# Working out the experts' order before the first expert stretch, and spreading the table steps behind it

## The chip, the cores and the metric

The kernel runs on one core of one Trainium2 chip. The time is device microseconds for one execution. A number given as the time of a kernel is the median of several executions; a profile is one execution with the hardware profiler on. Engines are named as the profile names them: PE (TensorE), DVE (VectorE), ACT (ScalarE), POOL (GpSimd), SP (SyncE). PEld is PE's weight load, which runs beside its matmuls.

## The reference, cut to what matters

Three layers follow one another. The first is attention with 2 batches, 8 heads, 768 tokens and 64 channels, where a query sees only keys of its own cluster. The second, which the change is in, is a mixture of 8 experts over N = 1536 tokens of D = 512 channels, one expert to a token. The third is a bilinear layer.

```python
logits = x @ w_gate
expert_idx = np.argmax(logits, axis=1)
...
for e in range(E):
    mask = expert_idx == e
    xe = x[mask]
    h = np.maximum(xe @ w1[e], 0.0)
    ye = h @ w2[e]
    out[mask] = gate_w[mask, None] * ye
...
a = x @ w_a
b = x @ w_b
return (a * b @ w_out)
```

## The kernel before, in words

**Attention, then routing.** The attention part runs unit by unit under a plan written out by hand. For each block of 128 tokens `route` finds every token's expert and its place among that expert's tokens, and keeps a running count per partition and expert in `run`. GpSimd scatters the rows of x by expert into `xs` in DRAM (`scatter`, L558). The last three blocks are not waited for: `place_mm` (L929) puts their rows of the first expert straight into PSUM (`x0t`) by matmuls with a matrix of places, beside the earlier rows, which sixteen matmuls with the identity add (L998).

**The expert stretches.** There are nine, in the order `SEQ` (L72) = 0, 1, 2, 7, 3, 8, 4, 5, 6. The numbers 0 to 6 are windows of up to 256 tokens of one expert, 7 is a tile of 128 rows for the expert with the fewest tokens, and 8 a tile of 128 rows for what an expert has beyond its window. A loop over the tiles that are left follows (L1301); it runs over none or some, by the counts. Which expert stands at which place is worked out on the chip by `tables` (L642): it sums `run` over partitions with one matmul (`cnt`), finds the expert with the fewest tokens, and writes `ri`: row 0 is the expert of each place, row 1 its first row in `xs`, row 2 its first column in the output `yt`. `wi` holds the same for stretch 8, `tab` the rest, and `aux` gets for each token's place its number and its gate, by twelve scatters of GpSimd (L779).

**A window** (`window`, L1088) computes h in eight blocks of 128 features, twelve matmuls each: the high and the low part of the weights with the high part of the input, and the high part with the low part of the input (`xh`, `xl`). Each block goes to a PSUM bank with the tag `h`, of which there are three. ACT rectifies it into `hh`, and DVE makes `hl`, the rest; then the bank is free. Then come eight blocks of y. A 128-row tile (`tile_of`, L1125) computes h with tokens on partitions in two banks, rectifies it into `hs` on ACT, and turns it by transposes (L1148) for its y.

**Weights.** Each expert's two matrices come in eight pieces of 512 KB. A piece is loaded by SP into one of four `raw` buffers (`piece_load`), cast by ACT into its high part `hi` and subtracted by DVE into its low part `lo` (`piece_parts`, L130); the load of piece n therefore waits for the `lo` of piece n - 4. There are twelve slots for parts. All queues work in the order in which the program issues.

**Ticks.** `tick` (L1203) is called sixteen times to a stretch, once to a block of h or y, and twice or once in a tile. At each tick it does one step of `tables` (a step ends at a `yield`), and splits pieces up to a number that leads the use by 6 pieces at first and by 10 at most. At tick 4 it calls `start_next(0)` (L1254): SP loads the expert numbers of the next two places from `ri` into registers, so that those weights can be loaded, and issues the load of the next window's rows, `xw`. The next window's transposes (`win_xt`, L1075), with `xh` by ACT and `xl` by DVE, are issued behind the y blocks that the last argument of `window` names. `load_ov` reads the output column from `ri` into registers of ACT and DVE at the second of these.

**PSUM.** With the expert stretches' pool (`mps`) the eight banks are: two for `xt`, two for `y`, three for `h`, one for the count (`rt`). In the last ticks of the stretches the pieces of the bilinear layer are split too. The bilinear stage begins with `split_y` (`yh`, `yl`), reads `aux`, and is bound by its matmuls.

Of the kernel before, what the change touches and what calls it, by code (L numbers as in the profile page):

```python
# [8 lines left out]
F32 = mybir.dt.float32  # L9
# [3 lines left out]
I32 = mybir.dt.int32  # L13
# [10 lines left out]
W = 256  # L24
# [5 lines left out]
def cluster_attention__then__moe__then__bilinear_kernel(  # L30
# [5 lines left out]
    DM, E = w_gate.shape  # L36
# [15 lines left out]
    NSLOT = NA + NB  # L52
# [8 lines left out]
    cp = pool(ctx, "const")  # L61
# [142 lines left out]
    ps = pool(st_aps, "attn_ps", space=PSUM)  # L204
# [434 lines left out]

    regs = {}  # L640

    def tables(rps, tp):  # L642


        tot = run[0]
        c = rps.tile([128, 512], F32, tag="rt", name="cnt")
        nc.tensor.matmul(c[:, 0:E], lhsT=ones, rhs=tot, start=True, stop=True)
        cnt = cp.tile([128, E], F32, name="cnts")
        nc.vector.tensor_copy(cnt, c[:, 0:E])

        m = cp.tile([128, 8], F32, name="wm")
        e1 = cp.tile([128, E], F32, name="we1")
        od = tp.tile([128, E], F32, name="od")
        nc.vector.tensor_reduce(out=m[:, 0:1], in_=cnt[:, 1:E], axis=AX.X, op=ALU.min)
        yield
        nc.vector.scalar_tensor_tensor(out=e1[:, 1:E], in0=cnt[:, 1:E], scalar=m[:, 0:1], in1=efirst[:, 0, 1:E],
                                       op0=ALU.is_le, op1=ALU.mult)
        nc.vector.tensor_reduce(out=m[:, 1:2], in_=e1[:, 1:E], axis=AX.X, op=ALU.max)
        yield
        nc.vector.tensor_scalar(out=m[:, 2:3], in0=m[:, 1:2], scalar1=-1.0, scalar2=float(E), op0=ALU.mult, op1=ALU.add)  # L660
        nc.vector.scalar_tensor_tensor(out=od, in0=ecol, scalar=m[:, 2:3], in1=ecol, op0=ALU.is_ge, op1=ALU.add)
        nc.vector.tensor_copy(od[:, E - 1:E], m[:, 2:3])
        yield
        ri = tp.tile([128, 3, E], I32, name="ri")
        nc.vector.tensor_copy(ri[:, 0, :], od)
        nc.vector.tensor_scalar(out=ri[:, 1, :], in0=od, scalar1=float(NTOK), scalar2=None, op0=ALU.mult)
        regs["ri"] = ri
        yield

        hot = tp.tile([128, E, E], F32, name="hot")  # L670
        t8 = tp.tile([128, E, E], F32, name="t8")
        o8 = tp.tile([128, 2, E], F32, name="o8")
# [58 lines left out]
        n = cp.tile([128, 2], F32, name="wn")  # L731
# [37 lines left out]
        for b in range(B):  # L769
            t = cp.tile([128, NT, E], F32, name=f"pt_{b}")  # L770
# [171 lines left out]
    for i in range(end + LAG):  # L942
# [31 lines left out]
        if i >= LAG:  # L974
            p, g, h, j = units[i - LAG]
# [19 lines left out]
    for d in range(DB):  # L995
        for a in range(2):
            o = W * (d % 2) + 128 * a
            nc.tensor.matmul(x0t[d // 2][:, o:o + 128], lhsT=x0[:, a, 128 * d:128 * d + 128], rhs=ident,  # L998
                             start=False, stop=False, skip_group_check=True)
    for d in range(DB):  # L1000
        place_mm(2, d)
    for t in range(NP):
# [14 lines left out]
    mp = pool(st_me, "moe")  # L1017
# [70 lines left out]
    def window(w, n, c0, tick, nxt, at):  # L1088
        hh, hl = [], []
        y = mps.tile([128, DB, W], F32, tag="y", name=f"y{w}")  # L1090
        for fb in range(FB):
            wh, wl = parts(c0 + fb // 2, DB)
            f0 = 128 * (fb % 2)
            hp_ = mps.tile([128, 512], F32, tag="h", name=f"h{w}_{fb}", bufs=3)
            seq = [(a_, xh[w], d) for d in range(DB) for a_ in (wh, wl)] + [(wh, xl[w], d) for d in range(DB)]
            for i, (a_, b_, d) in enumerate(seq):
                nc.tensor.matmul(hp_[:, 0:n], lhsT=a_[:, d, f0:f0 + 128], rhs=b_[:, d, 0:n],
                                 start=(i == 0), stop=(i == len(seq) - 1))
            th = mp.tile([128, W], F32R, tag=f"hh{fb}", name=f"hh{w}_{fb}")
            tl = mp.tile([128, W], F32R, tag=f"hl{fb}", name=f"hl{w}_{fb}")  # L1100
            nc.scalar.activation(out=th[:, 0:n], in_=hp_[:, 0:n], func=AF.Relu)
            nc.vector.scalar_tensor_tensor(out=tl[:, 0:n], in0=hp_[:, 0:n], scalar=0.0, in1=th[:, 0:n].bitcast(F32),
                                           op0=ALU.max, op1=ALU.subtract)
            hh.append(th)
            hl.append(tl)
            tick()
        for fb in range(FB):
            tick()
            wh, wl = parts(c0 + 4 + fb // 2, 2)
            for d in range(DB):  # L1110
                for i, (a_, b_) in enumerate(((wh, hh[fb]), (wh, hl[fb]), (wl, hh[fb]))):
                    nc.tensor.matmul(y[:, d, 0:n], lhsT=a_[:, fb % 2, 128 * d:128 * d + 128], rhs=b_[:, 0:n],  # L1112
                                     start=(fb == 0 and d % 2 == 0 and i == 0),
                                     stop=(fb == FB - 1 and d % 2 == 1 and i == 2), skip_group_check=True)
            if fb in at:
                nxt(at.index(fb))
        return y
# [6 lines left out]

    def tile_of(w, c0, tick, nxt, at):  # L1125

        hp_ = [mps.tile([128, 512], F32, tag="h", name=f"h{w}_{i}", bufs=3) for i in range(2)]
        hs = mp.tile([128, F], F32, tag="ys", name="hs", bufs=2)
        hh = [mp.tile([128, W], F32R, tag=f"hh{i}", name=f"sh{i}") for i in range(FB // 2)]
        hl = [mp.tile([128, W], F32R, tag=f"hl{i}", name=f"sl{i}") for i in range(FB // 2)]  # L1130

        def h_part(c):
            tick()
            tick()
            wh, wl = parts(c0 + c, DB)
            o = hp_[c // 2][:, 256 * (c % 2):256 * (c % 2) + 256]
            for d in range(DB):
                for i, (a_, b_) in enumerate(((xh[w], wh), (xl[w], wh), (xh[w], wl))):
                    nc.tensor.matmul(o, lhsT=a_[:, d, 0:WS], rhs=b_[:, d, :], start=(d == 0 and i == 0),
                                     stop=(d == DB - 1 and i == 2))  # L1140

        def h_split(i):
            nc.scalar.activation(out=hs[:, 512 * i:512 * i + 512], in_=hp_[i], func=AF.Relu)

        def h_turn(i):
            x = mps.tile([128, 512], F32, tag="xt", name=f"ht{i}", bufs=2)
            for j in range(4):
                nc.tensor.transpose(x[:, 128 * j:128 * j + 128], hs[:, 512 * i + 128 * j:512 * i + 128 * j + 128], ident)  # L1148
            for j in range(2):
                nc.scalar.copy(out=hh[2 * i + j], in_=x[:, W * j:W * j + W])  # L1150
            for j in range(2):
                nc.vector.tensor_tensor(out=hl[2 * i + j], in0=x[:, W * j:W * j + W],
                                        in1=hh[2 * i + j].bitcast(F32), op=ALU.subtract)

        y = mps.tile([128, DB, W], F32, tag="y", name=f"y{w}").rearrange("p d t -> p (d t)")[:, 0:512]

        def y_part(fb):
            tick()
            wh, wl = parts(c0 + 4 + fb // 2, 2)
            for i, (a_, b_) in enumerate(((hh, wh), (hl, wh), (hh, wl))):  # L1160
                nc.tensor.matmul(y, lhsT=a_[fb // 2][:, WS * (fb % 2):WS * (fb % 2) + WS], rhs=b_[:, fb % 2, :], start=(fb == 0 and i == 0),
                                 stop=(fb == FB - 1 and i == 2))

        h_part(0)
        h_part(1)
        h_split(0)
        h_part(2)
        h_turn(0)
        h_part(3)
        h_split(1)  # L1170
        y_part(0)
        y_part(1)
        h_turn(1)
        y_part(2)
        nxt(0)
        y_part(3)
        nxt(1)
        for fb in range(4, 8):
            y_part(fb)
        yn = mp.tile([128, F], F32, tag="ys", name="yn", bufs=2)[:, 0:DM]  # L1180
        nc.scalar.copy(out=yn, in_=y)

        def finish(a):
            if a:
                return
            x = mps.tile([128, 512], F32, tag="xt", name="yt_t", bufs=2)
            for d in range(DB):
                nc.tensor.transpose(x[:, 128 * d:128 * d + 128], yn[:, 128 * d:128 * d + 128], ident)
            store(x.rearrange("p (d t) -> p d t", d=DB), WS, at())

        return finish

    state = {"t": 0}
    LEAD = 6
# [8 lines left out]
    def tick():  # L1203
        t = state["t"]

        next(tab_steps, 0)
        if t == 4:
            start_next(0)
        n = t // 2 + min(LEAD + t // 8, NSLOT - 2)
        n64 = sum(t - T64 >= o for o in WHEN64)  # L1210
        if n64:
            split_ahead(MOE2 + n64)
        else:
            advance(min(n, MOE2), ENG)
        state["t"] += 1
# [12 lines left out]
    mps = pool(st_me, "moe_ps", space=PSUM)  # L1228

    mps.tile([128, 512], F32, tag="xt", name="xt_first", bufs=2)  # L1230

    tab_steps = tables(mps, mp)
    why = "computed here from counts that add up to the number of tokens"

    def sp_value(t, hi_, engines=(mybir.EngineType.SP,)):
# [30 lines left out]
    for pos, r in enumerate(SEQ):  # L1266
# [21 lines left out]
        if r >= E - 1:  # L1288
            finish = tile_of(r, 8 * pos, tick, nxt, lambda r=r: ov[r])
        else:  # L1290
            y = window(r, W, 8 * pos, tick, nxt, (1, 3) if pos else (3, 5))
            store(y, W, ov[r])
    keep_warm(2, "xt", [128, 512], 2, mps)
    st_me.close()
# [74 lines left out]
    for gr in range(NGR):  # L1369
        for st in range(NST):  # L1370
# [3 lines left out]
            for fl in range(GF + 1):  # L1374
                fb = GF * gr + fl
# [74 lines left out]
```

## Time and profile before

| | us |
|---|---|
| median of 3 runs | 791.07 |
| lowest and highest | 790.06, 794.5 |
| the profiled execution, its own time | 791.79 |
| its span, first to last instruction | 789.7 |
| PE busy in the span | 760.3 |
| DVE, ACT, POOL busy | 523.5, 356.5, 157.6 |

The span runs from the first to the last instruction of the profiled execution; what its own time has beyond that lies around it. Attention fills the span to about 264, the routing of the last rows to 279.4, the nine stretches to about 486, and the bilinear stage the rest. A matmul's busy time is that of a pipelined instruction, so busy shares near 100% only say that PE did not stand. An idle time is shown with what ended it.

### The profile page before, as it was taken

To read this page: it belongs to the slowest core of one execution; us is meant where nothing else is said; L and a number is where in the kernel's file an instruction comes from. 1 tells how busy PE (TensorE), PEld (TensorE's weight loads), DVE (VectorE), ACT (ScalarE), POOL (GpSimd) and SP (SyncE) were. 2 spreads that over 40 slices of the span, in tenths; PEclk is the share of its full clock that TensorE was granted. 3 is DMA by queue.
4 is the path that set the end of the run, shared out by engine and by line. 5 is a ranking of instruction groups with operands and counts; after the bars stand their busy time and mean duration, and the time that the engine had idled before them with its cause. 6 is when DMAs were issued, how large, how long until landed. Compare 5 with 4: busy or idle time off the path is not lost. (4 is left out here: it accounts for less than half of the span.)

```text
span 789.7 us, 12580 instructions
## 1 busy us (share of the span) xinstructions
PE 760.3 (96%) x4725; PEld 628.5 (80%) x4725; DVE 523.5 (66%) x947; ACT 356.5 (45%) x677; POOL 157.6 (20%) x164
## 2 busy tenths in 40 slices
PE   8999999999999897988999998999999999999996
PEld 8676667666666697988999998888888888888885
DVE  5867878768786768847776687756556665625323
ACT  6767667666675445447665532142331221211100
POOL 7623231414210410240000000321212111101011
PEclk9999999999999999999999999999999999999999
DMA  6585954846410157799777664323212220001011
GB/s 142 142 202 179 294 117 98 196 89 183 101 41 1 67 176 234 220 161 284 245 250 244 201 191 109 108 84 102 81 54 59 66 89 0 1 1 54 1 54 53
DMA packets 76302, 98.17 MB, mean 124 GB/s; under 512 B 28368, under 2 KB 49360, under 8 KB 76240
## 3 DMA queue, kind: packets, MB, share of 16 engines
q1 hardware_dynamic: 73792, 91.01, 41.9%
q0 software_dynamic: 2304, 6.31, 2.2%
q8 instruction: 38, 0.62, 0.3%
q14 instruction: 24, 0.20, 0.1%
q10 hardware_dynamic: 144, 0.03, 0.0%
HBM read 70.32 MB, written 10.50 MB: 102 GB/s over the span
## 5 line engine op out<-in xcount | busy, mean ns | idle before, releaser
L1387 PE MATMUL ab<-yh,hi 128*128 128x512 f32 x288 | 112.2, 389 | 2.5 <-ACT yh L1357 2.5
L1387 PE MATMUL ab<-yh,lo 128*128 128x512 f32 x288 | 112.1, 389 | 0.0
L1394 DVE TENSOR_TENSOR ga<-ga,ab 128x512 f32<-128x512 f32 x36 | 24.7, 686 | 126.1 <-PE ab L1387 92.5
L464 DVE TENSOR_REDUCE nm<-s 128x1 f32<-128x768 f32 x96 | 91.5, 953 | 19.0 <-PE s L462 13.9
L145 DVE TENSOR_TENSOR lo<-raw,hi 128x1024 fp32r<-128x1024 f32 x70 | 84.4, 1222 | 27.2 <-ACT hi L139 26.6
L145 POOL TENSOR_TENSOR lo<-tmp,hi 128x512 fp32r<-128x512 f32 x28 | 38.3, 1366 | 292.9 <-ACT hi L139 292.9
L471 ACT ACTIVATE pr<-s,nm 128x768 f32<-128x768 f32 x96 | 86.9, 906 | 18.4 <-DVE nm L464 16.3
L462 PE MATMUL s<-ks,qs 128*128 128x512 f32 (+1 forms) x384 | 91.4, 360 | 0.3 <-ACT pr L471 0.3
L1393 ACT COPY ga<-ab 128x512 f32<-128x512 f32 x36 | 21.1, 587 | 150.2 <-PE ab L1387 150.2
L485 PE MATMUL t<-ident,pr 128*128 128x128 f32 x576 | 82.7, 277 | 3.7 <-DVE pt L491 2.2
L485 PEld LDWEIGHTS t<-ident,pr 128*128 128x128 f32 x576 | 64.6, 141 | 24.4 <-issue 10.3
L139 ACT CAST hi<-raw 128x1024 fp32r<-128x1024 f32 x70 | 72.3, 1049 | 19.4 <-DMA raw<-in_moe_w 19.3
L1387 PE MATMUL ab<-yl,hi 128*128 128x512 f32 x288 | 77.2, 389 | 0.0
L501 PE MATMUL o<-pt,vn 128*64 128x384 f32 (+1 forms) x432 | 73.3, 462 | 0.0
L491 DVE COPY pt<-t 128x384 f32<-128x384 f32 x94 | 51.9, 552 | 24.9 <-PE t L485 24.6
L489 ACT COPY pt<-t 128x384 f32<-128x384 f32 x98 | 46.9, 479 | 44.9 <-PE t L485 43.7
L462 PEld LDWEIGHTS s<-ks,qs 128*128 128x128 f32 x384 | 58.4, 189 | 9.7 <-issue 4.4
L1387 PEld LDWEIGHTS ab<-yh,hi 128*128 128x128 f32 x288 | 54.1, 188 | 13.9 <-ACT yh L1357 2.7
L1112 PE MATMUL y<-hh,hi 128*128 128x256 f32 x224 | 63.5, 283 | 0.0
L1387 PEld LDWEIGHTS ab<-yl,hi 128*128 128x128 f32 x288 | 54.1, 188 | 11.6 <-DVE yl L1361 0.4
L1387 PEld LDWEIGHTS ab<-yh,lo 128*128 128x128 f32 x288 | 54.1, 188 | 11.2
L1112 PE MATMUL y<-hh,lo 128*128 128x256 f32 x224 | 62.6, 280 | 0.0
(328 smaller groups left out, 1548.5 us busy)
## 6 DMA issues: line engine op xcount, KB each, us to landing
raw<-in_moe_w SPq DMA_DIRECT2D x72, 512.0 KB, 4.6
raw<-in_moe_w_a SPq DMA_DIRECT2D x12, 512.0 KB, 3.6
raw<-in_moe_w_b SPq DMA_DIRECT2D x12, 512.0 KB, 3.7
raw<-in_moe_w_out SPq DMA_DIRECT2D x12, 512.0 KB, 3.7
qs<-hiq SPq DMA_DIRECT2D x14, 384.0 KB, 4.1
ks<-hik SPq DMA_DIRECT2D x28, 192.0 KB, 5.3
xs<-zero SPq DMA_DIRECT2D x8, 512.0 KB, 5.7
xw<-xs SPq DMA_DIRECT2D x14, 256.0 KB, 5.2
```

Source lines behind the costliest of these rows:

```text
L139: nc.scalar.copy(out=hi, in_=raw)
L145: eng.tensor_tensor(out=lo, in0=raw, in1=hi.bitcast(F32), op=ALU.subtract)
L462: nc.tensor.matmul(sc[:, c0:c1], lhsT=w, rhs=ks[s, h][:, i, c0:c1], start=(i == 0), stop=(i == 1))
L464: nc.vector.tensor_reduce(out=nm, in_=sc[:, 0:S], axis=AX.X, op=ALU.max, negate=True)
L471: nc.scalar.activation(out=pr, in_=sc[:, 0:S], func=AF.Exp, bias=nm, scale=1.0, accum_out=sums[p][:, t, h:h + 1])
L485: nc.tensor.transpose(x[:, 128 * n:128 * n + 128], pr[:, 128 * kb:128 * kb + 128], ident)
L489: nc.scalar.copy(out=dst, in_=src)
L491: nc.vector.tensor_copy(dst, src)
L501: nc.tensor.matmul(o[64 * h:64 * h + 64, 0:n], lhsT=vn[:, h, kb, :], rhs=pt_t[p, g, h][:, kb, 128 * j0:128 * j0 + n], start=(kb == 0), sto ...
L1112: nc.tensor.matmul(y[:, d, 0:n], lhsT=a_[:, fb % 2, 128 * d:128 * d + 128], rhs=b_[:, 0:n], start=(fb == 0 and d % 2 == 0 and i == 0), sto ...
L1387: nc.tensor.matmul(p_, lhsT=a_[:, d, f0:f0 + 128], rhs=b_[d], start=(i == 0), stop=(i == len(seq) - 1))
L1394: nc.vector.tensor_tensor(out=ga, in0=ga, in1=ab[1], op=ALU.mult)
```

## The change

`tables` takes its bank from the attention's pool (tag `T`) instead of the expert pool, and keeps `od` and `ri` in the constant pool. Its first four steps, from the count to `ri`, become one, which is issued ahead of the last block's `place_mm`; the other steps follow at ticks 2, 6, 10 and 14, then at each even tick from 18 to 46, and the rest (the places of `aux` and their twelve scatters) at each tick from 97 on, in the seventh stretch. `start_next(0)` is called at tick 0. The lead grows by one piece every 4 ticks where it was 8. Four banks carry the tag `h`. The first window asks for the next input's transposes behind its y blocks 1 and 3, where it was 3 and 5.

```diff
@@ -639,34 +639,32 @@
 
     regs = {}
 
-    def tables(rps, tp):
+    def tables(later):
 
 
         tot = run[0]
-        c = rps.tile([128, 512], F32, tag="rt", name="cnt")
+        c = ps.tile([128, 512], F32, tag="T", name="cnt", bufs=2)
         nc.tensor.matmul(c[:, 0:E], lhsT=ones, rhs=tot, start=True, stop=True)
         cnt = cp.tile([128, E], F32, name="cnts")
         nc.vector.tensor_copy(cnt, c[:, 0:E])
 
         m = cp.tile([128, 8], F32, name="wm")
         e1 = cp.tile([128, E], F32, name="we1")
-        od = tp.tile([128, E], F32, name="od")
+        od = cp.tile([128, E], F32, name="od")
         nc.vector.tensor_reduce(out=m[:, 0:1], in_=cnt[:, 1:E], axis=AX.X, op=ALU.min)
-        yield
         nc.vector.scalar_tensor_tensor(out=e1[:, 1:E], in0=cnt[:, 1:E], scalar=m[:, 0:1], in1=efirst[:, 0, 1:E],
                                        op0=ALU.is_le, op1=ALU.mult)
         nc.vector.tensor_reduce(out=m[:, 1:2], in_=e1[:, 1:E], axis=AX.X, op=ALU.max)
-        yield
         nc.vector.tensor_scalar(out=m[:, 2:3], in0=m[:, 1:2], scalar1=-1.0, scalar2=float(E), op0=ALU.mult, op1=ALU.add)
         nc.vector.scalar_tensor_tensor(out=od, in0=ecol, scalar=m[:, 2:3], in1=ecol, op0=ALU.is_ge, op1=ALU.add)
         nc.vector.tensor_copy(od[:, E - 1:E], m[:, 2:3])
-        yield
-        ri = tp.tile([128, 3, E], I32, name="ri")
+        ri = cp.tile([128, 3, E], I32, name="ri")
         nc.vector.tensor_copy(ri[:, 0, :], od)
         nc.vector.tensor_scalar(out=ri[:, 1, :], in0=od, scalar1=float(NTOK), scalar2=None, op0=ALU.mult)
         regs["ri"] = ri
         yield
 
+        tp = later()
         hot = tp.tile([128, E, E], F32, name="hot")
         t8 = tp.tile([128, E, E], F32, name="t8")
         o8 = tp.tile([128, 2, E], F32, name="o8")
@@ -997,6 +995,8 @@
             o = W * (d % 2) + 128 * a
             nc.tensor.matmul(x0t[d // 2][:, o:o + 128], lhsT=x0[:, a, 128 * d:128 * d + 128], rhs=ident,
                              start=False, stop=False, skip_group_check=True)
+    tab_steps = tables(lambda: mp)
+    next(tab_steps)
     for d in range(DB):
         place_mm(2, d)
     for t in range(NP):
@@ -1091,7 +1091,7 @@
         for fb in range(FB):
             wh, wl = parts(c0 + fb // 2, DB)
             f0 = 128 * (fb % 2)
-            hp_ = mps.tile([128, 512], F32, tag="h", name=f"h{w}_{fb}", bufs=3)
+            hp_ = mps.tile([128, 512], F32, tag="h", name=f"h{w}_{fb}", bufs=4)
             seq = [(a_, xh[w], d) for d in range(DB) for a_ in (wh, wl)] + [(wh, xl[w], d) for d in range(DB)]
             for i, (a_, b_, d) in enumerate(seq):
                 nc.tensor.matmul(hp_[:, 0:n], lhsT=a_[:, d, f0:f0 + 128], rhs=b_[:, d, 0:n],
@@ -1124,7 +1124,7 @@
 
     def tile_of(w, c0, tick, nxt, at):
 
-        hp_ = [mps.tile([128, 512], F32, tag="h", name=f"h{w}_{i}", bufs=3) for i in range(2)]
+        hp_ = [mps.tile([128, 512], F32, tag="h", name=f"h{w}_{i}", bufs=4) for i in range(2)]
         hs = mp.tile([128, F], F32, tag="ys", name="hs", bufs=2)
         hh = [mp.tile([128, W], F32R, tag=f"hh{i}", name=f"sh{i}") for i in range(FB // 2)]
         hl = [mp.tile([128, W], F32R, tag=f"hl{i}", name=f"sl{i}") for i in range(FB // 2)]
@@ -1203,10 +1203,12 @@
     def tick():
         t = state["t"]
 
-        next(tab_steps, 0)
-        if t == 4:
+
+        if t < 18 and t % 4 == 2 or 18 <= t < 48 and t % 2 == 0 or t >= 97:
+            next(tab_steps, 0)
+        if t == 0:
             start_next(0)
-        n = t // 2 + min(LEAD + t // 8, NSLOT - 2)
+        n = t // 2 + min(LEAD + t // 4, NSLOT - 2)
         n64 = sum(t - T64 >= o for o in WHEN64)
         if n64:
             split_ahead(MOE2 + n64)
@@ -1229,7 +1231,6 @@
 
     mps.tile([128, 512], F32, tag="xt", name="xt_first", bufs=2)
 
-    tab_steps = tables(mps, mp)
     why = "computed here from counts that add up to the number of tokens"
 
     def sp_value(t, hi_, engines=(mybir.EngineType.SP,)):
@@ -1288,7 +1289,7 @@
         if r >= E - 1:
             finish = tile_of(r, 8 * pos, tick, nxt, lambda r=r: ov[r])
         else:
-            y = window(r, W, 8 * pos, tick, nxt, (1, 3) if pos else (3, 5))
+            y = window(r, W, 8 * pos, tick, nxt, (1, 3))
             store(y, W, ov[r])
     keep_warm(2, "xt", [128, 512], 2, mps)
     st_me.close()
```

## Rows read from the trace of the kernel before

**Rows 1.** stages: length, busy PE, PEld, DVE, ACT, POOL, clock, DMA share, GB/s

```profile
264.00:279.40 15.40, 11.41 (x117) 10.11 (x115) 9.73 (x52) 5.74 (x15) 7.16 (x9) 1.00 0.33 106
279.40:374.00 94.60, 85.28 (x669) 82.74 (x670) 68.89 (x150) 50.64 (x76) 14.95 (x13) 0.96 0.79 219
374.00:490.00 116.00, 112.67 (x911) 110.08 (x911) 84.25 (x121) 60.73 (x99) 0.00 (x0) 1.00 0.68 213
...
415.00:419.00 4.00, 4.00 (x36) 4.00 (x35) 2.60 (x4) 2.11 (x5) 0.00 (x0) 1.00 0.95 288
```

**Rows 2.** PE waits, 276 to 490: total us, times, longest

```profile
PE h L1097 <- DVE hl L1102: 3.7, 5, 1.5
PE ab L1387 <- ACT yh L1357: 2.5, 1, 2.5
```

**Rows 3.** timeline of PE: start, us, instruction, [idle before <- what ended it]

```profile
269.63 0.48 PE L529 MATMUL xo<-iw,ot 128*128 128x144 f32 x2 [2.27 <-DVE sel L596]
...
309.29 0.74 PE L1097 MATMUL h<-xl,hi 128*128 128x256 f32 x4 [3.94 <-DVE xl L1086]
...
366.76 0.66 PE L1148 MATMUL ht<-ident,hs 128*128 128x128 f32 x4 [2.41 <-ACT hs L1143]
```

**Rows 4.** table of two-microsecond windows, columns as in rows 1

```profile
310.00:312.00 2.00, 2.00 (x12) 2.00 (x11) 1.87 (x5) 1.94 (x3) 0.00 (x0) 0.50 0.29 100
312.00:314.00 2.00, 2.00 (x14) 2.00 (x14) 1.75 (x6) 0.71 (x2) 0.00 (x0) 0.65 0.72 241
...
368.00:370.00 2.00, 2.00 (x10) 1.94 (x9) 2.00 (x4) 1.70 (x3) 0.00 (x0) 0.50 1.09 394
370.00:372.00 2.00, 2.00 (x10) 1.54 (x8) 0.73 (x1) 1.11 (x2) 0.00 (x0) 0.65 0.99 353
```

**Rows 5.** timeline of DVE, columns as in rows 3

```profile
276.74 1.22 DVE L145 TENSOR_TENSOR lo<-raw,hi 128x1024 fp32r<-128x1024 f32 x1
279.48 1.29 DVE L1224 TENSOR_TENSOR xl<-x0t,xh 128x512 fp32r<-128x512 f32 x2 [1.52 <-ACT xh L1222]
...
284.28 0.42 DVE L1102 SCALAR_TENSOR_TENSOR hl<-h,hh 128x256 fp32r<-128x256 f32 x1
284.61 0.16 DVE L649 COPY cnts<-cnt 128x8 f32<-128x8 f32 x1
...
288.04 0.16 DVE L666 TENSOR_SCALAR ri<-od 128x8 int32<-128x8 f32 x1
...
308.54 0.69 DVE L1086 TENSOR_TENSOR xl<-xt,xh 128x512 fp32r<-128x512 f32 x1 [0.49 <-DVE wcum L728]
```

**Rows 6.** timeline of ACT, columns as in rows 3

```profile
295.62 1.05 ACT L139 CAST hi<-raw 128x1024 fp32r<-128x1024 f32 x1 [4.43 <-DMA raw<-in_moe_w]
...
355.77 1.05 ACT L139 CAST hi<-raw 128x1024 fp32r<-128x1024 f32 x1 [4.36 <-DMA raw<-in_moe_w]
...
365.17 1.04 ACT L139 CAST hi<-raw 128x1024 fp32r<-128x1024 f32 x1 [1.65 <-DMA raw<-in_moe_w]
```

**Rows 7.** timeline of SP's DMA issues, columns as in rows 3

```profile
277.99 4.50 SPq L102 DMA_DIRECT2D raw<-in_moe_w  x2
289.58 0.93 SPq L1073 DMA_DIRECT2D xw<-xs  x2
```

**Rows 8.** DMA issues, 340 to 344: operation, count, KB, us to landing

```profile
raw<-in_moe_w SPq DMA_DIRECT2D x3, 512.0 KB, 13.7
```

**Rows 9.** the page's DMA issues, whole span

```profile
raw<-in_moe_w SPq DMA_DIRECT2D x72, 512.0 KB, 4.6
```

**Rows 10.** timeline of POOL, first and last of the twelve scatters

```profile
329.32 0.97 POOL L779 DMA_INDIRECT aux<-auxt,pu  x1 [49.22 <-DVE pu L777]
...
347.94 0.97 POOL L779 DMA_INDIRECT aux<-auxt,pu  x1 [0.30 <-issue]
```

**Rows 11.** timeline of PE around the first stretch's start

```profile
275.77 2.03 PE L998 MATMUL x0t<-ident,zero 128*128 128x128 f32 x16
...
280.52 0.81 PE L1097 MATMUL h<-xl,hi 128*128 128x256 f32 x4
```

## The prediction

> **What bounds it now.** I read the table of stages first. The reader is to see that the matrix engine (PE) is the bound nearly everywhere, and that what it loses lies in one place: between 279.4 and 374 it is busy 85.28 of 94.60 us with a mean granted clock of 0.96, in the stretch behind 112.67 of 116 us at full clock [rows 1]. So 9.3 us of idle time and some 3.5 us of slow clock lie in the first expert stretches, 3.3 us in the later ones, of which 2.5 us is the hand-over to the last stage (yh) [rows 2], which the change doesn't touch. No cheaper matmul is on offer; all that can be won is these waits.
>
> Next the PE's waits and, in its timeline, the two large ones. PE waited 3.94 us until 309.29 for the low part of the second stretch's input (xl), and 2.41 us until 366.76 for the rectified h of the 128-row tile (hs) [rows 3]. Five waits for hl, which frees a bank for h, make 3.7 us [rows 2]. Behind each of the two large ones the granted clock stands at 0.50 for two microseconds and at 0.65 for two more, that is, mostly at the lower of its two levels, 1.2 GHz, until it is back at 2.4: 2 x 0.50 + 2 x 0.35 = 1.7 us of work lost each time, PE being busy throughout [rows 4]. A gap of 2.27 us in the attention stage has no such fall behind it, in a stage with clock 1.00 [rows 1, 3]; I use it only as a sign that a gap of one microsecond costs no clock.
>
> Then what is late behind each. **The wait at 309.** The xl that ended it began on VectorE (DVE) at 308.54 [rows 5], behind the tables' small instructions and the lo parts of weights. Those lo parts were late: ScalarE (ACT) had stood 4.43 us, until 295.62, for a weight load [rows 6]. That load was late because SyncE (SP) issued nothing between the last load of the first expert (two loads, 277.99 to 282.49) and 289.58, when ri, the experts' order, had come (DVE wrote it at 288.04 to 288.20) [rows 5, 7]. **The wait at 367.** ACT stood 4.36 us until 355.77 and 1.65 us until 365.17 for weight loads, with hs behind them in its queue [rows 6]. Three loads issued between 340 and 344 took 13.7 us (median) [rows 8], where the median of all 72 is 4.6 [rows 9]; GpSimd was issuing the twelve scatters of aux then, 329.32 to 348.91 [rows 10].
>
> **The change, part by part.**
>
> 1. Order ahead of the first stretch. The count's matmul now stands behind the 16 matmuls that begin at 275.77 and end at 277.80 by the model [rows 11]. PE has to do these anyway, and run, which it reads, comes just ahead of the lo at 276.74 [rows 5], so PE pays under 0.1 us. On DVE the nine instructions from cnts to ri come ahead of that lo, and so ahead of xl0, now at 279.48 [rows 5]. The first and the last of the nine take 0.16 each [rows 5]; with the gap that each leaves to the next one that needs it, I put the nine at 1.75 us. Start 277.75, end 279.5; lo 1.22, to 280.7; xl0 1.29, to 282.0 instead of 280.77. PE wants xl0 at 280.52 [rows 11], takes its two halves as they come, and ends its first block 1.1 us late. Bounds: 0.9 (no gaps between the nine) and 1.6 (the count half a microsecond later); no gain, since xl0 can only come later. I take **+1.1**, with no clock lost [rows 3]. The two loads that wait for lo parts here are issued up to 2.7 us later: they carry the first expert's second half, and ACT comes to them only behind three h blocks; if that cover went, hh would be late, which the fourth bank takes up.
>
> 2. Loads of later experts start earlier. SP passes its two loads (the second at about 283.2, when the next lo is done), waits for no order any more, and needs for the register loads and the two xw what it needed from 288.20 to 290.51, 2.3 us [rows 5, 7]. So it comes to the second expert's weights at 285.5 instead of 290.5, 5 us earlier, and ACT's 4.43 us go. The input's transposes are asked for two blocks of y earlier. With the tables at every fourth tick, DVE has for each tick at most 0.75 of a lo (1.22), one hl (0.42) [rows 5] and a quarter of a step, near 1.4 us, where an h block of twelve matmuls takes 1.3 (36 in 4 us) [rows 1]; the four banks carry the difference. I reckon xl done near 301, some 3 us before PE wants it. So the wait goes, with its clock: **-3.94 - 1.7 = -5.6**. Bounds: 0 and -5.6. Next late is nothing: PE is.
>
> 3. A fourth bank for h, from the space of the count's bank. Each of the five waits was for the hl three blocks back; now it is for the one four back. The worst is 1.5 us [rows 2], where several hl came one behind another, and half a microsecond of it may stay. **-3.7 + 0.5 = -3.2**; bounds -3.7 and -1.5 (each shortened, none gone).
>
> 4. Tables at ticks 14 to 46, the last steps from 97 on. All instructions stay; they leave DVE's fullest stretch. The store's address (ri's third row) is ready at tick 10 and read at tick 11 by ACT and DVE; what stands behind it is the second half of the next input. Cost: 0, covered by PE's y half, which needs neither; without that cover, one lo, 1.2 us. tab's load on SP moves some twenty ticks later, with its data long there: 0.
>
> 5. The twelve scatters move from 329-349 into the seventh stretch, about 415 to 435 by the count of ticks, behind both 128-row tiles. GpSimd is idle there. The loads that lay beside them are quick again, ACT reaches hs in time, and the wait at 367 goes: **-2.41 - 1.7 = -4.1**. The second 128-row tile lies between 374 and 490, where 3.3 - 2.5 = 0.8 us is all of PE's wait [rows 1, 2]; so a tile without scatters has no such wait, and I take it whole. Bounds 0 and -4.1. At the new place the loads already keep the queues 0.95 busy, at 288 GB/s [rows 1]. ACT may again stand 4.4 us [rows 6], but in a 256-row stretch, where three blocks in the banks are 3.9 us of cover. I take **0**, and keep +1.7 to +4.1 for the range: half of the stall with no clock, or the whole as it was.
>
> 6. The deeper lead (t // 4 for t // 8, up to the same 10) adds no instruction; its pull on DVE is in part 2. 0.
>
> **Sum**: 1.1 - 5.6 - 3.2 - 4.1 = -11.8, on the profiled execution's own 791.79 us (span 789.7): 780.0. The median of the runs, 791.07, is 0.7 below that execution, so I forecast **779.3** for the median.
>
> **Rivals.** A (0.59): the forecast, with the bounds of parts 1 and 3 and the 1.0 us by which a run went below its median: 777.5 to 782.
>
> B (0.22): the scatters bring their stall along. For: the 13.7 us loads beside them, and queues nearly full at the new place. Against: no 128-row tile follows, and a window's h rides on four banks. The loads are slow until ACT needs them in the eighth stretch's h half; +1.7 to +4.1 gives 781.0 to 783.4.
> The Trainium skill's page "DMA: Bandwidth & Descriptors", section "Issuing engines are not separate DMA queues", says that transfers started by different engines run on the same sixteen DMA engines and interleave. By that rule moving the scatters cures nothing, it moves the slowness, and B would be the case; the trace agrees as far as 13.7 us against 4.6 goes, and does not show which of ACT's waits PE would feel.
>
> C (0.13): the early order starts nothing early, so that the change doesn't do what it says. SP takes its work in order, the xw loads wait for the last rows' scatter, and four raw buffers allow a load only when the lo four before is done, on a DVE that now starts 1.2 us later. If the second expert's weights come as late as now, part 2 gives nothing: 779.3 + 5.6 = 784.9.
>
> D (0.06): no gain, or slower. Place: the loads beside the scatters in the seventh stretch, behind which the last stage's first weights come. Price: each batch of six holds loads up by 13.7 - 4.6 = 9.1 us; if PE felt both, and fell to the lower clock behind each, 18.2 + 3.4 = 21.6, it would end at 800.9, slower than before. It decides once PE feels 11.8 of these 21.6. Against: the same slowness cost PE only 4.1 us here, with three banks.
>
> **How the numbers follow.** Faster by over 0.5% (4 us, about what a measurement of this kernel can tell) is under 787.1: A, B, C whole or in part, 0.89 after what C and A may miss. Within: D half felt, and a C with more lost, 0.08. Slower: 0.03. The range goes from A's lower end over B to C, 777.5 to 785.0, and leaves out C's upper part and D.
>
> **What would show it.** Right: cnts on DVE near 277.8 and ri before 280; a PE wait of about 1 us for xl0 near 281; SP's first xw near 285; no PE wait for xl near 305 and none for hs; hl waits under 1 us together; clock 1.00 from 300 to 380; aux scattered from about 405 on, since all is 10 us earlier by then. Wrong: ACT waits for raw in the seventh and eighth stretch with PE waits behind them (B), a gap near 305 with a late load ahead of it (C), or a longer wait at the last stage's start (D).

## The result and the profile after

The changed kernel takes 781.79 us in the median (780.73 to 784.55, four executions), the kernel before on the same chip 790.57 (789.46 to 794.5): a ratio of 0.9888, with a 95% interval of 0.9857 to 0.992. That is 8.8 us less; the forecast was 11.8 less, to 779.3, with a range of 777.5 to 785.0. In the two profiled executions it is 791.79 to 781.50, 10.3 less. The waits in the expert stretches changed as forecast; the clock did not.

The stages first, against [rows 1]. Everything is some 10 us earlier by the end of the first four stretches, so the row that ended at 374 ends at 364 now.

```profile
279.40:364.00 84.60, 83.52 (x679) 81.97 (x680) 69.59 (x136) 52.83 (x79) 0.38 (x1) 1.00 0.76 246
364.00:478.00 114.00, 111.00 (x899) 108.79 (x898) 83.13 (x129) 58.60 (x96) 14.30 (x12) 1.00 0.78 215
```

PE's idle time is 1.1 us in the first and 3.0 us in the second, where it was 9.3 and 3.3, and the clock of the first stands at 1.00 for 0.96. PE's waits in the stretches, against [rows 2, 3]:

```profile
PE ab L1388 <- ACT yh L1358: 2.5, 1, 2.5
...
PE h L1097 <- DVE xl L1226: 0.7, 1, 0.7
PE h L1097 <- DVE hl L1102: 0.4, 1, 0.4
PE xt L1082 <- issue: 0.3, 1, 0.3
```

The waits for xl of the second stretch and for hs are gone, those for hl are 0.4 us for 3.7, and 0.7 us is new: the first stretch's xl. Summed with the unchanged wait for xh (0.7), it is 4.6 us where it was 13.2.

Why the new wait is there, and how small it is, stands on DVE, against [rows 5]:

```profile
277.70 0.17 DVE L649 COPY cnts<-cnt 128x8 f32<-128x8 f32 x1 [1.03 <-PE cnt L647]
...
279.31 0.16 DVE L663 TENSOR_SCALAR ri<-od 128x8 int32<-128x8 f32 x1
279.43 1.23 DVE L145 TENSOR_TENSOR lo<-raw,hi 128x1024 fp32r<-128x1024 f32 x1
280.58 1.28 DVE L1226 TENSOR_TENSOR xl<-x0t,xh 128x512 fp32r<-128x512 f32 x2
...
300.74 0.68 DVE L1086 TENSOR_TENSOR xl<-xt,xh 128x512 fp32r<-128x512 f32 x1
```

The count comes to DVE at 277.70, ri ends at 279.47, the lo that stood at 276.74 stands at 279.43, and xl follows at 280.58 instead of 279.48. PE waits for its first half, and for its second between its matmuls (1.10 us for the four, where they took 0.81 [rows 11]):

```profile
281.31 1.10 PE L1097 MATMUL h<-xl,hi 128*128 128x256 f32 x4 [0.69 <-DVE xl L1226]
```

And the other end of the same move, on SP, against [rows 7]:

```profile
280.69 2.70 SPq L102 DMA_DIRECT2D raw<-in_moe_w  x2
284.86 0.93 SPq L1073 DMA_DIRECT2D xw<-xs  x2
286.04 20.48 SPq L102 DMA_DIRECT2D raw<-in_moe_w  x12
```

xw goes out at 284.86 instead of 289.58, and the second expert's weights from 286.04 on. The second stretch's xl is done at 301.4, in the last row of DVE above; it was 309.2. ACT still stands for those weights, but 1.91 us where it was 4.43 [rows 6], and no one behind it is in need. In the later stretches its longest wait is 1.79 us:

```profile
291.44 1.05 ACT L139 CAST hi<-raw 128x1024 fp32r<-128x1024 f32 x1 [1.91 <-DMA raw<-in_moe_w]
...
436.09 1.05 ACT L139 CAST hi<-raw 128x1024 fp32r<-128x1024 f32 x1 [1.79 <-DMA raw<-in_moe_w]
```

The scatters, against [rows 10], are at 410 to 428 now, and the slow loads [rows 8] went with them; those issued between 424 and 428 take 13.2 us (median, the second fence), and the four other windows of four microseconds between 412 and 432 show 7.8 to 11.7 us:

```profile
410.29 0.97 POOL L777 DMA_INDIRECT aux<-auxt,pu  x1 [130.51 <-DVE pu L775]
...
427.56 0.97 POOL L777 DMA_INDIRECT aux<-auxt,pu  x1 [0.30 <-issue]
```

```profile
raw<-in_moe_w SPq DMA_DIRECT2D x2, 512.0 KB, 13.2
```

So the slowness moved with its cause, and PE did not feel it at the new place. The Trainium skill's page "DMA: Bandwidth & Descriptors", section "Issuing engines are not separate DMA queues", has transfers started by the sync and the gpsimd engine run on the same DMA engines and interleave. The trace agrees as far as SP's loads take 13.2 us beside GpSimd's scatters; it doesn't show where the two meet.

What is not as forecast is the clock. Behind the hand-over to the bilinear stage, which the change doesn't touch, the granted clock falls to its lower level now. Before, it did not:

```profile
477.05 0.50 PE L1388 MATMUL ab<-yh,hi 128*128 128x512 f32 x1 [2.54 <-ACT yh L1358]
```

```profile
478.00:480.00 2.00, 2.00 (x7) 1.54 (x6) 2.00 (x4) 0.00 (x0) 0.00 (x0) 0.50 0.33 5
480.00:482.00 2.00, 2.00 (x8) 1.59 (x7) 1.39 (x3) 0.31 (x1) 0.00 (x0) 0.67 0.00 0
```

That is 2 x 0.50 + 2 x 0.33 = 1.7 us. One more such loss lies in the attention stage of this execution, in code that is the same in both kernels, behind a gap of 1.33 us. The kernel before has the same gap, and the clock stood at 1.00 behind it:

```profile
190.68 0.55 PE L485 MATMUL t<-ident,pr 128*128 128x128 f32 x3 [1.33 <-DVE pt L491]
```

```profile
190.00:200.00 10.00, 9.32 (x52) 6.24 (x52) 7.60 (x14) 4.69 (x11) 3.90 (x4) 0.83 0.49 165
```

The books of the two profiled executions: waits in the stretches -8.6; the gap of 2.27 us at 269.63 [rows 3] that is 0.37 here, -1.9; two falls of the clock gone, -3.4; two others come, +3.4. Sum -10.5, measured -10.3. The -1.9 is not the change's: that gap is 2.2 to 2.3 us in nine of the fourteen traces here, of both kernels (2.26 in another trace of the changed kernel), and 0.37 in the five others, which are this one and the four of the first session below.

### The profile page after: what moved, and what is told of

It reads as the page before. It is cut to its first block, busy times and chain, and to the rows that moved or that the text cites. A ratio compares the mean times of both kernels' runs of the same rounds, so it can differ in the third digit from the quotient of the medians.

```text
span 779.4 us, 12578 instructions
## 1 busy us (share of the span) xinstructions
PE 760.5 (98%) x4725; PEld 629.1 (81%) x4725; DVE 523.8 (67%) x947; ACT 356.2 (46%) x677; POOL 157.1 (20%) x164
```

## The experiments

Twelve runs, in three sessions on different chips. The kernel before takes 790.7, 793.7 and 794.8 us in these, so only times of one session, or ratios, are compared. A ratio, with its 95% interval, is an estimate from the executions of a session and need not be the quotient of the two medians.

**Three banks.** The bank alone undone.

```diff
-            hp_ = mps.tile([128, 512], F32, tag="h", name=f"h{w}_{fb}", bufs=4)
+            hp_ = mps.tile([128, 512], F32, tag="h", name=f"h{w}_{fb}", bufs=3)
...
```

> The changed kernel with three banks for h in place of four. If the bank removed the hl waits (as forecast), they come back: between 1.5 and 3.7 us of PE waits for hl in all, among them some in the eighth stretch, where ACT stood up to 1.9 us for loads beside the scatters; 783.3 to 785.5 us. If the spread tables had removed them and the bank is incidental, hl waits stay under 0.7 us together, as with four banks: 781.8 to 782.3 us.

Measured: 783.21 us (780.46 to 784.64), ratio 0.9905 (0.9883 to 0.9927). By time it can't be told from the changed kernel. By PE's waits it can:

```profile
PE h L1097 <- DVE hl L1102: 2.1, 2, 1.7
```

Two waits instead of one, 2.1 us instead of 0.4: in this execution the bank is worth 1.7 us in the changed kernel, most of it one wait in the last stretch (1.7, at 455.5), and none of it in the eighth, where it was expected. The other 1.6 of the 3.7 us of before were not the bank's.

**Four banks in the kernel before.** The reverse of it.

```diff
-        c = rps.tile([128, 512], F32, tag="rt", name="cnt")
+        c = rps.tile([128, 512], F32, tag="xt", name="cnt", bufs=2)
...
-            hp_ = mps.tile([128, 512], F32, tag="h", name=f"h{w}_{fb}", bufs=3)
+            hp_ = mps.tile([128, 512], F32, tag="h", name=f"h{w}_{fb}", bufs=4)
...
```

> The kernel before with four banks for h (the count takes a bank of the transposes), nothing else. If the bank is worth what was forecast, hl waits fall from 3.7 to under 0.7 us together, and the time by about 3 us, to 787.6. If DVE is simply behind in those stretches, the microseconds come back in the waits for xl and hs, which grow: 790 to 791 us.

Measured: 794.09 us against 793.7, ratio 0.998 (0.9953 to 1.0008).

```profile
PE h L1097 <- DVE xl L1086: 4.3, 1, 4.3
PE ht L1148 <- ACT hs L1143: 3.0, 1, 3.0
PE h L1097 <- DVE hl L1102: 1.2, 1, 1.2
PE y L1161 <- DVE sl L1152: 0.8, 1, 0.8
```

hl waits fall from 3.7 to 1.2, and what they gave comes back: xl 4.3 for 3.9, hs 3.0 for 2.4, 0.8 for sl, which PE had not waited for. Alone the bank gives nothing that can be measured. By these waits DVE was behind, and a buffer more doesn't make it catch up.

**Scatters early.** The changed kernel with gates, places and scatters as a generator of their own, at ticks 20 to 37.

```diff
+        regs["off"] = off
...
+    def places():
+        off = regs["off"]
         yield from gates(B - 1, True)
...
+        if t >= 20:
+            next(place_steps, 0)
```

> The changed kernel with the twelve scatters of aux (and the gates and places before them) issued at ticks 25 to 37 as in the kernel before, all else as changed. If the scatters made the wait for hs, loads issued beside the second six take over 9 us again, ACT stands over 3 us for them, and PE waits 1.5 to 2.5 us for hs in the first 128-row tile, with a fall of the clock behind it in most executions: 783.3 to 785.9 us. If that wait came of the late order and the dense tables ahead of it, nothing returns: no wait for hs over 0.3 us, 781.8 us.

Measured: 784.53 us, with four executions from 780.54 to 788.48, ratio 0.9899 (0.9863 to 0.9934); the profiled one is the longest. By time it can't be told from the changed kernel (0.9857 to 0.992).

```profile
PE xt L1085 <- issue: 4.2, 1, 4.2
...
PE ht L1151 <- ACT hs L1146: 1.2, 1, 1.2
PE xt L1085 <- DMA xw<-xs: 1.0, 1, 1.0
...
PE y L1164 <- DVE sl L1155: 0.3, 1, 0.3
```

hs is only 1.2 of 6.7 us. The largest wait is for a bank of transposes, and its chain is in the timeline: ACT stands 3.70 us for a weight load; behind it come `sh` and DVE's `sl`, which read the bank until 367.06, and PE starts as it is free.

```profile
364.09 1.04 ACT L139 CAST hi<-raw 128x1024 fp32r<-128x1024 f32 x1 [3.70 <-DMA raw<-in_moe_w]
365.04 0.64 ACT L1153 CAST sh<-ht 128x256 fp32r<-128x256 f32 x2
...
366.31 0.75 DVE L1155 TENSOR_TENSOR sl<-ht,sh 128x256 fp32r<-128x256 f32 x2
...
367.16 1.08 PE L1085 MATMUL xt<-ident,xw 128*128 128x128 f32 x4 [4.22 <-issue]
```

Because the four executions lay so far apart, it ran again, beside the changed kernel on one chip.

> The changed kernel itself, as the mark for the three beside it. Its executions differ by how often the clock falls behind gaps of 1.8 to 3 us: between none, about 780.5 us, and three, about 785 us.

> The changed kernel with the scatters at ticks 25 to 37, again, beside the changed kernel on one chip, since its four executions lay 8 us apart. If the scatters there hold up the 128-row tile's weights, PE waits 2 us or more for hs, for the tile's transposes or for xw in the profile, and the median is 2 to 4 us above the changed kernel. If the first time was chance, within 1 us of it.

Measured: the changed kernel 781.33 us (779.0 to 784.77), ratio 0.9855 (0.9823 to 0.9887); scatters early 786.85 (784.36 to 788.75), ratio 0.9912 (0.9878 to 0.9945). 5.5 us between the medians, more than the 2 to 4 expected; the two sets of six executions meet only between 784.36 and 784.77.

```profile
PE xt L1085 <- issue: 1.3, 2, 1.2
PE y L1164 <- DVE sl L1155: 0.8, 1, 0.8
...
PE ht L1151 <- ACT hs L1146: 0.5, 1, 0.5
```

2.6 us of waits in and around the same 128-row tile, by another split. So the place of the scatters is what makes that tile's weights late; which of the tile's steps then stands differs between the two traces. These waits don't make the 5.5 us: the profiled execution (785.48) also has two falls of the clock ahead of the expert stretches, behind the gaps at 190 and at 271, in code that this edit doesn't touch, and that of the changed kernel (779.0) has none before the last 10 us.

**Scatters late in the kernel before.**

```diff
-        next(tab_steps, 0)
+        if t < 24 or t >= 97:
+            next(tab_steps, 0)
```

> The kernel before with only the places and the twelve scatters of aux moved to tick 97 and later. If the scatters made the wait for hs, it is gone (under 0.3 us) with its clock, and the waits for xl and hl stay: 2.4 to 4.1 us less than before, 786.5 to 788.2 us. If moved scatters only move their stall, PE waits as much in the seventh or eighth stretch, where three banks stand for h: 790 to 791 us.

Measured: 789.96 us against 793.7, ratio 0.9944 (0.9921 to 0.9968): 3.7 less.

```profile
PE h L1097 <- DVE xl L1086: 4.4, 1, 4.4
...
PE h L1097 <- DVE hl L1102: 1.5, 2, 1.1
...
PE xt L1082 <- DVE yt L1121: 0.6, 1, 0.6
PE y L1112 <- issue: 0.4, 1, 0.4
```

No hs among the waits, xl as before. In the new place, with three banks for h, PE waits 0.4 and 0.6 us at 424 and 429, and no more. Of all parts, this one has its price most clearly.

**Order late.** Everything as changed but the order, at tick 3 with its count in a bank of the transposes, its loads at tick 4 and the first window's requests for transposes behind y blocks 3 and 5.

```diff
-        c = ps.tile([128, 512], F32, tag="T", name="cnt", bufs=2)
+        c = mps.tile([128, 512], F32, tag="xt", name="cnt", bufs=2)
...
-    next(tab_steps)
...
-        if t < 18 and t % 4 == 2 or 18 <= t < 48 and t % 2 == 0 or t >= 97:
+        if t == 3 or 3 < t < 18 and t % 4 == 2 or t == 9 or 18 <= t < 48 and t % 2 == 0 or t >= 97:
             next(tab_steps, 0)
-        if t == 0:
+        if t == 4:
             start_next(0)
...
-            y = window(r, W, 8 * pos, tick, nxt, (1, 3))
+            y = window(r, W, 8 * pos, tick, nxt, (1, 3) if pos else (3, 5))
```

> The changed kernel with the order worked out at tick 3 and its loads started at tick 4, the input's transposes behind y blocks 3 and 5 as before; tables still spread, four banks, scatters late. If the late loads made the wait for xl at 309 (the forecast's step), SP's first xw is near 289 again, ACT stands 4 us for the load behind it, and PE waits 2 to 4 us for xl near 305, with the clock: 784 to 787 us. If the tables' instructions on DVE made it, xl is in time: PE waits for it under 1 us, and the 1.1 us for xl0 is saved: 780.7 to 782 us.

Measured: 787.35 us (786.15 to 789.0), ratio 0.996 (0.9945 to 0.9976).

```profile
295.58 1.05 ACT L139 CAST hi<-raw 128x1024 fp32r<-128x1024 f32 x1 [9.28 <-DMA raw<-in_moe_w]
```

```profile
307.81 0.58 PE L1096 MATMUL h<-xh,hi 128*128 128x256 f32 x1 [4.68 <-ACT xh L1084]
```

ACT stood 9.28 us for the load, from 286.30 on, where the kernel before asked for it at 291.19 and got it at about the same time (the deeper lead asks sooner); xh came late rather than xl, and PE waited 4.68 us, with the clock at 0.76 and 0.90 in the two stretches of 10 us around. SP's first xw went out at 287.85. Against the changed kernel's ratios (0.9888, and 0.9855 in a later session) 0.996 is 5.7 to 8.3 us more. The wait and its clock are back whole, without the tables' crowd on DVE: the late order is enough to make it. Whether its late weights or the later transposes of the input do it isn't shown apart.

**Tables dense.** The order early, but a step at every tick to 18.

```diff
-        if t < 18 and t % 4 == 2 or 18 <= t < 48 and t % 2 == 0 or t >= 97:
+        if t < 19 or t >= 97:
```

> The changed kernel with a step of the tables at every tick from 0 to 18, the order still early. If the late loads made the wait for xl, dense tables cost little: PE waits for xl and hl under 1.5 us together, 781.8 to 783.3 us. If the tables' instructions on DVE made it, PE waits 2 to 4 us for xl near 305: 784 to 787 us.

Measured: 786.88 us (784.49 to 787.73), ratio 0.9942 (0.992 to 0.9963).

```profile
PE h L1097 <- DVE hl L1102: 3.3, 2, 2.6
...
PE h L1097 <- DVE xl L1086: 1.8, 1, 1.8
```

1.8 us for the second stretch's xl and 3.3 for hl (the longer, 2.61, at 317), where the changed kernel has none and 0.4, and four banks didn't prevent it; by the ratios 4.3 to 6.9 us more. Crowding DVE is enough too. So neither theory holds alone: the early order and the spread tables each take away one of two sufficient causes. With either of them undone, what is left of the whole change (0.996 and 0.9942) is no better than the late scatters alone in the kernel before (0.9944), so the rest of the gain comes only with both. The lead (t // 4 for t // 8) wasn't tried by itself; both runs have the deeper one, and whether either cause is enough without it isn't shown.

**The order behind the first xl.** Two tries to save the 1 us that the nine instructions cost.

```diff
         nc.tensor.matmul(c[:, 0:E], lhsT=ones, rhs=tot, start=True, stop=True)
+        yield
         cnt = cp.tile([128, E], F32, name="cnts")
         nc.vector.tensor_copy(cnt, c[:, 0:E])
...
+    next(tab_steps)
     advance(NA + NRAW, ENG)
```

> The changed kernel with the count's matmul where it is and the nine instructions of the order on DVE moved behind the first stretch's xl. If the 1.1 us for xl0 was their whole price, PE's 0.7 us wait goes and the second half comes at once, 1.0 us less: 780.8 us; ri comes near 282.5 instead of 279.5, SP's xw no later than now, since SP has its last load of the first expert to issue until then. If the later order costs, SP's xw comes after 286 and a wait for xl or hl grows by 0.5 us or more: 781.3 us or more.

Measured: 782.5 us against 793.7, ratio 0.9849 (0.9803 to 0.9894).

```profile
280.65 0.15 DVE L650 COPY cnts<-cnt 128x8 f32<-128x8 f32 x1
...
280.95 0.36 PE L1098 MATMUL h<-xh,hi 128*128 128x256 f32 x1 [2.26 <-DVE cnts L650]
```

PE now waited 2.26 us for the copy of the count: the first h block's bank is the bank that the count was summed in, and it is free only when DVE has read it. The clock fell behind this gap (0.83 from 280 to 290). The second try puts the copy, one instruction, ahead of xl and the other eight behind it:

```diff
+        yield
         nc.vector.tensor_copy(cnt, c[:, 0:E])
+        yield
...
     advance(NA + AN, ENG)
+    next(tab_steps)
...
+    next(tab_steps)
     advance(NA + NRAW, ENG)
```

> The changed kernel with the lo part first, then the copy of the count, then the first stretch's xl, and only then the other eight instructions of the order on DVE. The copy comes before PE asks for the bank of the count, which held PE up by 2.3 us in the earlier try. If the nine cost PE 1 us by standing ahead of xl, the wait for xl near 281 is gone and the first block is whole, 0.9 to 1.0 us less than the changed kernel. If ri, now near 282.5, is then late for SP, the first xw moves past 286 and the time is the changed kernel's or more.

Measured: 781.1 us (780.18 to 782.53) beside the changed kernel's 781.33; ratio 0.9841 (0.9812 to 0.987).

```profile
279.63 1.29 DVE L1229 TENSOR_TENSOR xl<-x0t,xh 128x512 fp32r<-128x512 f32 x2 [1.37 <-ACT xh L1227]
```

```profile
286.16 0.39 PE L1099 MATMUL h<-xh,hi 128*128 128x256 f32 x1 [0.37 <-DVE hl L1104]
```

xl is back at 279.63 and PE doesn't wait for it; a wait of 0.37 us for hl takes part of its place, and xw goes out half a microsecond later, at 285.38. The price of the nine, 1 us by the trace, is real, but what is won can't be told from noise.

**Matmuls in the hand-over.**

```diff
-    keep_warm(2, "xt", [128, 512], 2, mps)
+    keep_warm(8, "xt", [128, 512], 2, mps)
```

> The changed kernel with eight matmuls with the identity behind the last stretch instead of two, at the hand-over to the bilinear stage, where PE stood 2.54 us and the clock stood at 0.50 behind it in the profiled execution. If that fall makes part of what was missing to the forecast, PE stands under 2 us there, the clock is 1.00 behind it, and the time is 0 to 1.7 us lower, about 780.8 in the median. If the fall has nothing to do with the gap, the clock falls there as often and the time is 781.8; if PE gets through the added matmuls too late, up to 0.5 us more.

Measured: 782.13 us against 793.7, ratio 0.9833 (0.9789 to 0.9876).

```profile
477.32 1.14 ACT L1358 CAST yh<-yt 128x512 fp32r<-128x512 f32 x2 [1.64 <-PEq L1302]
...
478.93 0.50 PE L1388 MATMUL ab<-yh,hi 128*128 128x512 f32 x1 [2.14 <-DVE yl L1362]
```

The clock stayed at 1.00 behind it in the profiled execution, but PE still stood 2.14 us: in the changed kernel it begins 0.67 us behind the start of yh (476.38 to 477.05), here 1.61, 0.9 us later than yh would have let it. The likely reason, argued and not shown, is that PE goes through the branch over the left-over tiles only when the added matmuls are out. With four instead of eight, on top of the second try above:

> The same with four matmuls with the identity behind the last stretch instead of two. Eight kept PE from the bilinear stage for some 0.9 us, since PE needed about 2 us from the last of them to its first matmul there; four end about 0.5 us later than two, which the wait for yh covers. If the shorter gap there keeps the clock up more often, 0 to 0.8 us less than without in the median; if not, no difference.

Measured: 781.79 us (780.4 to 782.45), ratio 0.9847 (0.9818 to 0.9875). PE stood 2.13 us and the clock fell all the same (0.86 and 0.97 in the two stretches of 10 us). No gain, and no version here that is measurably better than the change.

## Why the prediction was right, and where it wasn't

The direction, the range and the list of what the profile would show held; the time came out 2.5 us above the forecast. It lies in the ranges of both A and B, so it is PE's waits and not the time that speak for A. In the later session the changed kernel's ratio is 0.9855, where the forecast's 779.3 to 791.07 is 0.985: there it is met.

1. **xl0, +1.1.** Measured 0.69 + 0.29 = 1.0, with count, ri and xl within 0.2 us of where the text put them. Right, and confirmed by the second try, where the wait goes.

2. **Early loads, -5.6.** The wait is gone, and the late order alone brings it back whole. The size is right, the reason is half of it: the text named the loads as the cause, and counted the tables at every fourth tick only into DVE's work per tick. Dense tables bring 4.3 to 6.9 us back with the loads early. Part 4 priced the spreading at **0**; the runs show that part 2's gain hangs on it.

3. **Fourth bank, -3.2.** hl waits fell by 3.3, but the step that gave it to the bank failed: three banks bring 1.7 back, and four banks in the kernel before gain nothing measurable. That a wait moves to the hl "four back" helps only if DVE isn't behind for longer than a block. What took the other 1.6 us, the spread tables, the early order or both, wasn't tried for hl apart; with dense tables alone the hl waits are back at 3.3 us. That the sum came out is in part luck.

4. **Scatters, -4.1 and 0 at the new place.** -3.7 in the kernel before, 2.6 to 6.7 us of waits back in the changed one. B named the mechanism rightly (loads of 7.8 to 13.2 us where the scatters are), and the cover held: three blocks of h in banks against ACT waits of 1.8 us.

5. **The clock, -3.4 in all.** This is the term that was mis-sized. It took each of the two falls as bound to its wait, and the hand-over, an unchanged gap of 2.5 us with no fall behind it, as free. For gaps of this length a fall comes in some executions and not in others (below). The long wait for xl did carry its 1.7; the 2.4 us for hs carried it in that execution, and the hand-over carried one in the next. The sign taken from the gap of 2.27 us, that a gap of one microsecond costs no clock, fails too: the clock fell behind that gap in three of the nine traces that have it, and behind one of 1.33 us in four of fourteen. In the profiled pair the terms of the forecast themselves came to -8.6 + 0.3 (the rest of xl0) - 3.4 = -11.7, beside the forecast's -11.8; what separates this from the measured -10.3 is the -1.9 and the two new falls, +3.4, outside of the expert stretches. For the medians, falls in other executions are the likely reason and not a shown one: the execution of the changed kernel with the highest mean clock (0.999, too high for one whole fall) took 780.73, near the 780.0 that the sum gave ahead of its step to the median.

C fell with xw at 284.86. B's stall and D fell with PE's waits: none is listed in the seventh and eighth stretch, and the hand-over is 2.54 us where it was 2.52.

## What to carry to other kernels

A wait that ends on one engine can have two sufficient causes, here a late order with its loads and a crowded vector engine; undo each alone before you share out a gain, and expect the parts not to add up. A buffer more covers jitter, not an engine that is behind. Work that slows transfers without a computing engine of its own did least harm here where what is loaded beside it has slack, and where the stage's engines have buffers to run on; one such place was tried.

## What the runs showed of the hardware that was not expected

**Behind one and the same short gap of PE the clock falls in some executions and not in others.** The hand-over gap, 2.1 to 2.6 us, is in all fourteen traces. Behind it the granted clock fell to the lower level in six (the changed kernel's first, scatters early's first, scatters late and four banks in the kernel before, the second try, and the one with four matmuls) and stayed at 1.00 in eight. Shorter gaps do it too: the one of 1.33 us at 190, in all fourteen traces, has a fall behind it in four, and that of 2.2 to 2.3 us at 270 in three of nine. A gap of 2.95 us (hs, four banks before) had no fall behind it, nor had one of 2.61 (hl, dense tables); one of 1.84 (xl, dense tables) had one. The five waits of 3.9 us or more all had. One fall costs 1.7 us where PE is at work all through it. In four of the five long waits the clock fell while PE still stood, stayed low for longer behind them, and cost 2.1 to 2.9 us. What decides whether it falls wasn't found. A forecast should give a gap of about 2 us a part of the price, by how often it was seen (6 of 14 and 3 of 9 here), and not all of it or nothing.

**Scattered pairs of 8 bytes slow the loads beside them more than their own traffic explains.** The same stretch of time, 322 to 352, in the changed kernel and, below it, with the scatters early in it:

```profile
q1 hardware_dynamic: 4499, 5.57, 59.4%
raw<-in_moe_w SPq DMA_DIRECT2D x11, 512.0 KB, 3.7
```

```profile
q1 hardware_dynamic: 3766, 4.89, 92.8%
q0 software_dynamic: 384, 0.01, 1.1%
raw<-in_moe_w SPq DMA_DIRECT2D x10, 512.0 KB, 9.5
```

The columns of the queues are packets, MB and the time that the packets took, as a share of the 16 DMA engines' time. The scatters' queue, q0, moves 0.01 MB and takes 1.1%. Yet the queue of the loads, q1, takes 92.8% of that time for 4.89 MB, where it took 59.4% for 5.57 MB, and a load takes 9.5 us (median) instead of 3.7. Beside the scatters elsewhere (412 to 432 in the changed kernel, 340 to 344 in the kernel before) the loads take 7.8 to 13.7 us. What in the DMA path holds the loads wasn't found.
